# Splitting the first projection by columns and reordering the start of an attention-plus-gMLP kernel

## The chip, the cores and the metric

The kernel runs on one core of a Trainium2 chip. The metric is the device time of one execution in microseconds (us). A core has five engines that run their own instruction streams: TensorE (PE; its weight loads are shown apart as PEld), VectorE (DVE), ScalarE (ACT), GpSimd (POOL) and SyncE (SP). Here SP and POOL mostly issue transfers; ACT issues a few as well.

## The reference

The input `x` has 2048 rows of 1024 bf16 numbers. Two blocks follow each other: sliding attention, and a gated MLP that also mixes over the rows.

```python
h  = x + A(layernorm(x), wqkv, wo)
h2 = h + B(layernorm(h), w_in, w_sp, b_sp, w_out)

def A(x, wqkv, wo):                       # 32 heads of 32
    q, k, v = split(x @ wqkv)
    idx  = pos[:, None] - 2 * arange(8)   # 8 keys per row, two rows apart, looking back
    logits = einsum('bhsd,bhswd->bhsw', q, k[idx]) * 32 ** -0.5   # idx < 0 masked
    o = einsum('bhsw,bhswd->bhsd', softmax(logits), v[idx])
    return o @ wo

def B(x, w_in, w_sp, b_sp, w_out):
    z1, z2 = halves(gelu(x @ w_in))       # 1792 columns each
    z2 = layernorm(z2)
    g  = w_sp @ z2 + b_sp[:, None]        # 2048 x 2048, mixes rows
    return (z1 * g) @ w_out
```

## The kernel before

**Tiling.** The rows are worked in four chunks of 512 (`CH`), each of four tiles of 128 rows (`TPC`). A matmul contracts over 128 partitions, so 1024 columns are eight slices (`KT`), and a 128x512 matmul fills half of a PSUM accumulator `acc` (three of them; one more PSUM region, `L`, belongs to attention). Q, k and v are computed transposed (columns of wqkv on the partitions, rows of x along the free axis): a chunk of q is 64 matmuls in four accumulators of 16. Column `m*8+dl` of q goes to partition `m`, slice `dl`, so the weights of a matmul are read with a stride of eight columns.

**Stages.** In the first (up to about 438 us) the chunks pass through LN1, q/k/v, attention, the wo projection with the residual and LN2 (`head`), and the two halves of the gelu projection (`b_z2`, `b_z1`), interleaved. In the second, z2 of all 16 tiles sits in SBUF, and per chunk there are the spatial product with w_sp (L810) and the projection by w_out (L825).

**What sets the order.** From `qkv(0)` on, nearly every piece of work of the first stage is handed to `Order` (L63, used as `o_` from L282) as an operation with an engine, an estimated duration, its dependencies and a priority; `take` and `free` name buffers. `Order.run` simulates the engines with these estimates and then emits the operations in the order of their simulated starts, so it fixes each engine's instruction order. A "DMA" operation is either a transfer to be issued (by SP, `dma`, or by POOL, `dma_w`) or a mere delay. What comes ahead of that (the start, L206 to L271) is placed by the framework's own scheduler. Each engine, and each queue of transfers, then works its stream in order and waits for semaphores.

**The start.** PE runs 14 warm-up matmuls on a zeroed tile (L207, L210). Tiles 0 and 3 of x are loaded by SP and ACT (L214: SP loads 0 and 3, ACT 1 and 2), then wq in eight slices (L217), wk (L218), x of chunk 1 by tiles (L220), wv (L221) and x of chunks 2 and 3 (L223), all on SP. DVE takes mean and variance of tiles 0, 1, 2 (`stats`, L227 to L229), ACT those of tile 3 by two sums over the tile (`stats_act`, L234/L235, finished on DVE, L236 to L238); ACT takes the root (L242), DVE the reciprocal (L243) and the normed tile (`norm`, L247). PE turns a tile by eight 128x128 transposes into PSUM (L255), and one copy of 128x1024 brings it to `xnT[0]` (L256; ACT, but DVE for tile 2). Then q of chunk 0: the first 32 matmuls go over the slices `kt` on the outside and four column groups on the inside, in two accumulators (L346), the other 32 are normal groups (L355); ACT brings accumulators out (L362).

**LN1 of chunks 1 to 3** (`ln1`, L294): statistics on DVE, `rstd` by a power on POOL (L303), four norms on DVE, each stored to a buffer `xn_d` in DRAM by POOL's queue (L309); then one DMA transpose on SP from `xn_d` to `xnT[c]` (L315). Matmuls of q, k, v follow (L355); ACT copies each accumulator to a staging tile (L367), and SP stores it to `qkv_d` in DRAM.

**Attention** (`attention`, L378). POOL's queue loads `qT`, `kT` and `vT` of the chunk from `qkv_d` (L387; chunk 0 has them in SBUF), kT and vT with 16 rows of the chunk before. The load of qT waits for `qfree` of the chunk before, that of kT for `qkdone`, that of vT for `avdone`. For each of eight windows DVE multiplies qT with the shifted kT (L414, into one of two buffers `prod`) and adds slices up (L418, L421, L424) into `part`. After four windows PE sums over each head's partitions with four matmuls into `L` (L442, at most one half of `L` a visit), so there are two visits a chunk. Softmax is on DVE and ACT (L451 to L485), PE spreads the weights over the partitions again (`pb`, L497), copies bring them to `AB` (L502). DVE multiplies v with AB for each window (L517) and adds (L525); two of the sums are done by accumulating transfers on POOL's queue (`gather`, L531), `av_y<-av_z` and `av_oT<-av_zz`. The product `z` is kept in the buffer of qT (`homes`, L508), so `qfree` is the end of the first of these transfers (L536).

**Head and gMLP.** `head`: wo projection (L587), residual with x loaded once more (`xr`, L591; L596), squares (L601), LN2 (L629), and a DMA transpose of the normed tiles `hb` on SP into `hnT` (L634; for the last chunk by tiles, L619). `b_z2` (L660) and `b_z1` (L710) are matmuls that depend only on `hnT` and on weights; where no attention work is ready for PE, `Order` puts them there.

Of the kernel before, what the change touches and what calls it, by code (L numbers as in the profile page):

```python
# [20 lines left out]
P = 128  # L21
NT = S // P
# [10 lines left out]
NWARM = 14  # L33
# [4 lines left out]
ACCUM_US = 12.0  # L38
PIECES = ((0, 0), (0, 4), (1, 0), (1, 4))
LNPRIO = (0, 2.0, 2.5, 4.0)  # L40
# [86 lines left out]
def kernel(  # L127
# [18 lines left out]

    consts_d = nc.inline_tensor(_consts(), name="qt_consts")
# [6 lines left out]
    xn_d = {c: dpool.tile([CH, D], BF16, name=f"xn_d{c}") for c in (1, 2, 3)}  # L154
# [9 lines left out]
    V.memset(eps_t[:], EPS)  # L164
    texp = cpool.tile([P, 1], FP32, name="texp")
    nhalf = cpool.tile([P, TPC], FP32, name="nhalf")
    V.memset(nhalf[:], -0.5)
# [34 lines left out]
    def load_x(i):  # L202
        x_slot(i)
        dma(xts[i], x2d[i * P:(i + 1) * P, :])
# [4 lines left out]
    for _ in range(NWARM):  # L209
        T.matmul(wps[:], warm[:, 0:P], warm[:], start=True, stop=True)  # L210

    for i in (0, 3, 1, 2):
        x_slot(i)
# [17 lines left out]
    def stats_act(i):  # L231
        sm = l1.tile([P, 4], FP32, name="sm", tag="sm")
        jk = l1.tile([P, D], BF16, name="jk", tag="xn", bufs=4)
        A.activation(jk[:], xts[i], ACTF.Identity, accum_out=sm[:, 0:1])  # L234
        A.activation(jk[:], xts[i], ACTF.Square, accum_out=sm[:, 1:2])  # L235
# [4 lines left out]
    def rstd_of(lo, hi):  # L240
# [4 lines left out]
    def norm(i):  # L245
        xn = l1.tile([P, D], BF16, name="xn", tag="xn", bufs=4)
        V.tensor_scalar(xn[:], xts[i], mv1[:, i, 0:1], rstd1[:, i:i + 1], op0=ALU.subtract, op1=ALU.mult)  # L247
        return xn

    xnT[0] = xtp.tile([P, KT, CH], BF16, name="xnT", tag="xnT")  # L250

    def xpose(i, xn):
        tp = ps_acc.tile([P, KT, P], BF16, name="tpa", tag="acc")
        for a in range(KT):
            T.transpose(tp[:, a, :], xn[:, a * P:(a + 1) * P], ident)  # L255
        (V.tensor_copy if i == 2 else A.copy)(xnT[0][:, :, i * P:(i + 1) * P], tp[:])  # L256
# [3 lines left out]
    stats_act(3)  # L260
    stats(V, 0)
    rstd_of(0, 1)
    stats(V, 1)
    xpose(0, norm(0))
    rstd_of(1, 2)
    rstd_of(3, 4)
    xpose(1, norm(1))
    xpose(3, norm(3))
    stats(V, 2)
    rstd_of(2, 3)  # L270
    xpose(2, norm(2))  # L271
# [10 lines left out]
    o_ = Order({"PE": 12.9, "ACT": 12.0, "DVE": 12.6, "POOL": 12.0}, {"acc": 3, "L": 1, "prod": 2, "part": 2, "xn": 4})  # L282
# [8 lines left out]
    X_AT = {1: 18.5, 2: 27.5, 3: 30.5}  # L291
    xn_ready = {}

    def ln1(c):  # L294
        sts = []
        for i in range(c * TPC, (c + 1) * TPC):
            arrive = add("DMA", X_AT[c] + 0.8 * (i % TPC), lambda: None)
            sts.append(add("DVE", 1.32, lambda i=i: stats(V, i), [arrive], prio=LNPRIO[c]))
# [572 lines left out]
```

## Time and profile before

| what | value |
|---|---|
| median of 3 runs | 732.07 us (731.43 to 734.21) |
| the profiled execution | 734.07 us, of which the span from first to last instruction 732.2 |
| granted TensorE clock, mean | 0.995 |
| DVE, ACT, POOL busy | 419.3 (57%), 220.8 (30%), 59.0 (8%) us |
| from 0 to 28.64 us (to the end of chunk 0's q) | PE busy 24.57, at a mean granted clock of 0.88; DMA share 0.96, 350 GB/s |
| from 28.64 to 438.70 (rest of the first stage) | PE busy 408.33 of 410.06; DVE 329.31; DMA share 0.69 |
| from 438.70 to the end | PE busy 290.30 of 293.50; DVE 73.49; ACT 1.02; DMA share 0.27 |
| HBM read, written | 55.09 MB, 33.88 MB |

The profiled execution is 2.0 us above the median of the runs; all positions in the trace belong to it. The stages differ: in the last one almost only PE works, and what a change does there is a shift of the whole; up to 28.64 us PE has unoccupied time and a lowered clock; in between, PE and DVE both have long streams that meet at a few places in each chunk.

### The profile page before, as it was taken

What the parts mean: (1) busy time and instruction counts of PE and PEld (TensorE: products, weight loads), DVE (VectorE), ACT (ScalarE), POOL (GpSimd) and SP (SyncE); (2) the same over time, 40 slices, a digit from 0 to 9 for tenths busy, and PEclk for the clock granted to TensorE, in tenths of its full rate; (3) what the DMA queues carried; (4) which work ended last, traced back from release to release, by engine and by line L of the source; (5) the groups of instructions that cost most, each with busy time, mean ns of one, the idle gap of its engine ahead of it and who ended that gap; (6) DMA issues with size and microseconds to landing.
All of it is one profiled execution on the core that took longest, in us unless ns stands there. A gap on an engine that the chain in (4) does not pass through costs nothing.

```text
span 732.2 us, 8410 instructions
## 1 busy us (share of the span) xinstructions
PE 723.2 (99%) x3452; PEld 367.1 (50%) x3452; DVE 419.3 (57%) x464; ACT 220.8 (30%) x269; POOL 59.0 (8%) x74
## 2 busy tenths in 40 slices
PE   7999999999999999999999999999999999999998
PEld 3666665566645344444444444444444444444444
DVE  4889999999899899989940101322232223222322
ACT  4322522544238874678654620000000000000000
POOL 0310110001201110201203000000000000000000
PEclk8999999999999999999999999999999999999999
DMA  9874398476993485383569898344105311020002
GB/s 338 311 263 112 124 235 253 145 187 204 317 372 66 150 214 166 101 233 64 123 195 295 191 283 259 111 114 131 58 30 127 117 57 42 22 90 21 1 16 71
DMA packets 115398, 113.64 MB, mean 155 GB/s; under 512 B 67904, under 2 KB 91872, under 8 KB 115232
## 3 DMA queue, kind: packets, MB, share of 16 engines
q1 hardware_dynamic: 105472, 72.63, 33.9%
q0 software_dynamic: 9456, 39.89, 18.7%
q8 instruction: 27, 0.44, 0.2%
q10 hardware_dynamic: 432, 0.59, 0.2%
q14 instruction: 11, 0.09, 0.0%
HBM read 55.09 MB, written 33.88 MB: 122 GB/s over the span
## 4 chain that ended last, share of the span: by engine, by line
PE 89%; DMA 5%; DVE 4%; issue 1%; ACT 0%; DVEq 0%
PE acc L810 26%; PE acc L355 18%; PE acc L825 13%; PE acc L710 13%; PE acc L660 10%; PE acc L587 6%; DMA qT<-qkv_d 2%; DVE prod L414 2%; DMA qkv_d<-stg 2%; PE acc L346 1%; DMA xr<-in_A_x_dram 1%; DVE prod L418 1%; DVE prod L421 0%; DMA xp<-in_A_x_dram 0%; PE tpa L255 0%
## 5 line engine op out<-in xcount | busy, mean ns | idle before, releaser
L810 PE MATMUL acc<-wspT,z2sb 128*128 128x512 bf16 x896 | 194.0, 379 | 0.0
L810 PEld LDWEIGHTS <-z2sb 128*128 128x128 bf16 x896 | 87.7, 98 | 105.7
L813 DVE TENSOR_TENSOR g<-acc,bB 128x1024 bf16<-128x1024 f32 x28 | 34.3, 1224 | 160.2 <-PE acc L810 127.6
L660 PE MATMUL acc<-win,hnT 128*128 128x512 bf16 (+1 forms) x512 | 98.5, 352 | 0.0
L710 PE MATMUL acc<-hnT,win 128*128 128x512 bf16 x448 | 98.4, 379 | 0.0
L414 DVE TENSOR_TENSOR prod<-qT,kT 128x4096 bf16<-128x4096 bf16 x32 | 72.5, 2283 | 5.2 <-ACT kT L362 2.9
L660 PEld LDWEIGHTS <-hnT 128*128 128x128 bf16 x512 | 49.8, 98 | 47.3 <-issue 0.7
L825 PEld LDWEIGHTS <-zg 128*128 128x128 bf16 x462 | 45.2, 98 | 51.8
L710 PEld LDWEIGHTS <-win 128*128 128x128 bf16 x448 | 43.4, 98 | 52.4 <-issue 1.1
L367 ACT CAST stg<-acc 128x1024 bf16<-128x1024 f32 x36 | 36.4, 1011 | 72.7 <-PE acc L355 59.2
L825 PE MATMUL acc<-wout_a,zg 128*128 128x512 bf16 (+1 forms) x264 | 58.2, 373 | 0.0
L832 DVE TENSOR_TENSOR ot<-acc,hr 128x1024 bf16<-128x1024 f32 x15 | 18.4, 1225 | 69.4 <-PE acc L825 69.4
L355 PE MATMUL acc<-xnT,wv 128*128 128x512 bf16 x256 | 56.6, 380 | 0.0
L355 PE MATMUL acc<-xnT,wk 128*128 128x512 bf16 x256 | 56.3, 379 | 0.0
L587 PE MATMUL acc<-wo_sb,av_oT 128*128 128x512 bf16 x256 | 55.9, 379 | 0.0
L355 PE MATMUL acc<-xnT,wq 128*128 128x512 bf16 x224 | 49.7, 380 | 0.0
L355 PEld LDWEIGHTS <-wk 128*128 128x128 bf16 x256 | 36.5, 144 | 18.8 <-issue 0.5
L355 PEld LDWEIGHTS <-wv 128*128 128x128 bf16 x256 | 36.5, 144 | 18.8 <-issue 0.7
L825 PE MATMUL acc<-wout_b,zg 128*128 128x512 bf16 (+1 forms) x198 | 44.4, 373 | 0.0
L587 PEld LDWEIGHTS <-av_oT 128*128 128x128 bf16 x256 | 25.1, 98 | 30.1
L355 PEld LDWEIGHTS <-wq 128*128 128x128 bf16 x224 | 31.9, 144 | 16.4 <-issue 0.7
L418 DVE TENSOR_TENSOR prod<-prod 128x2048 bf16<-128x2048 bf16 x32 | 38.3, 1216 | 0.0
(135 smaller groups left out, 565.0 us busy)
## 6 DMA issues: line engine op xcount, KB each, us to landing
qkv_d<-stg SPq DMA_DIRECT2D x36, 256.0 KB, 3.2
z_d<-z1s SPq DMA_DIRECT2D x28, 256.0 KB, 3.5
z1c<-z_d SPq DMA_DIRECT2D x28, 256.0 KB, 2.6
z_d<-u SPq DMA_DIRECT2D x12, 448.0 KB, 4.2
z2sb<-z_d POOLq DMA_DIRECT2D x12, 448.0 KB, 15.6
xr<-in_A_x_dram SPq DMA_DIRECT2D x16, 256.0 KB, 2.8
av_y<-av_z POOLq DMA_DIRECT2D x4, 1024.0 KB, 10.0
av_oT<-av_zz POOLq DMA_DIRECT2D x4, 1024.0 KB, 13.4
```

What stands on the lines that cost most here:

```text
L346: T.matmul(accs[dl // 2][:, dl % 2, :], wv[:, kt, dl, :], xnT[0][:, kt, :], start=(kt == 0), stop=(kt == KT - 1))
L355: T.matmul(G[key][:, j, :], wv[:, kt, dl, :], xnT[c][:, kt, :], start=(kt == 0), stop=(kt == KT - 1))
L367: A.copy(stg[:], G[key][:])
L414: V.tensor_tensor(st["prod"][:], qT[:], kT[:, :, o:o + CH], op=ALU.mult)
L418: V.tensor_tensor(dst, p_[:, 0:4, :], p_[:, 4:8, :], op=ALU.add)
L587: T.matmul(st["acc", il][:, nh, :], oTs[c][:, dl, il * P:(il + 1) * P], wo_sb[:, dl, nh * CH:(nh + 1) * CH], start=(dl == 0), stop=(dl == ...
L660: T.matmul(accf[:, n0:n1], hnTs[c][:, il, kt, :], wins[hf][:, kt, n0:n1], start=(kt == 0), stop=(kt == KT - 1))
L710: T.matmul(G["accy", c, fp][:, j, :].rearrange("p (a b) -> p a b", a=TPC), wt[:, kt, f0 * P:(f0 + 1) * P], hnTs[c][:, :, kt, :], start=(kt ...
L810: T.matmul(acc[:, j, :], z2sb[a][:, f * P:(f + 1) * P], wspT[:, a, :], start=(a == 0), stop=(a == NT - 1))
L813: V.tensor_tensor(g1[:], acc[:], bB[:, c * CH:(c + 1) * CH].unsqueeze(1).to_broadcast([P, 2, CH]), op=ALU.add)
L825: T.matmul(outs, zg[:, f, il * P:(il + 1) * P], wt[:, f0, lo:hi], start=(f == 0), stop=(f == NF - 1))
L832: V.tensor_tensor(ot[:], acc[:].rearrange("p a b -> p (a b)"), hr[:], op=ALU.add)
```

## The change

The start is written out by hand for all engines, and some of the later work is placed differently.

- **Start.** 20 warm-up matmuls in place of 14. Tiles 0 and 1 of x are loaded in column halves, one by SP and one by ACT; tile 2 by SP, tile 3 by ACT. Each tile's transposes go to a PSUM region of its own, and its copy out is two 128x512 copies by one engine: even tiles ACT, odd tiles DVE. For the first 32 matmuls of q, the left half of the rows (tiles 0 and 1) is done by 128x256 matmuls before tiles 2 and 3 are turned, the right half after that; the other 32 are full ones. `xnT` is laid out by tiles.
- **Loads of x.** Chunks 1 and 2 come in pairs of tiles, two pairs ahead of wk and two behind it; chunk 3 comes in one load (`xl`) ahead of wv, into a buffer of the products (`prod`), so `Order` starts with one `prod` buffer and gets the other when chunk 3's norms are done.
- **LN1 of chunks 1 to 3.** The normed tiles go to a buffer `xns` in SBUF, and the DMA transpose reads that; `xn_d` and its stores are gone. The buffers `hn0` and `hn1` are shared by `xns`, `hnT` and the product `z`; `xns` of chunk 3 takes the one of chunk 1 and waits for its transpose. ACT sums tiles 7 and 11, finished on DVE.
- **Head sums.** `part` holds all eight windows; eight matmuls in one visit of PE per chunk.
- **Product z.** Chunks 0 and 1 keep it in `hn1`, so the next chunk's qT is loaded once the products with qT are done (`qkdone`).
- **The planner's numbers.** Starts of the engines, arrival times of x, due times of the accumulating transfers (11 and 15 in place of 12), some durations and priorities.

```diff
-NWARM = 14
+NWARM = 20
...
-ACCUM_US = 12.0
 PIECES = ((0, 0), (0, 4), (1, 0), (1, 4))
-LNPRIO = (0, 2.0, 2.5, 4.0)
+LNPRIO = (0, 2.0, 2.5, 2.8)
...
+    by_hand = tc.manual_schedule(engines={mybir.EngineType.PE, mybir.EngineType.Activation, mybir.EngineType.DVE, mybir.EngineType.Pool})
+    by_hand.__enter__()
...
-    xn_d = {c: dpool.tile([CH, D], BF16, name=f"xn_d{c}") for c in (1, 2, 3)}
...
+    def load_pair(k):
+        x_slot(2 * k)
+        x_slot(2 * k + 1)
+        dma(pairs[k][:], x2d[2 * k * P:(2 * k + 2) * P, :].rearrange("(t p) d -> p t d", p=P))
...
-    for i in (0, 3, 1, 2):
-        x_slot(i)
-        (dma if i < 2 else A.dma_start)(xts[i], x2d[i * P:(i + 1) * P, :])
...
-    for kt in range(KT):
-        dma(wsb[0][:, kt, :], wq_view[:, kt, 0:D])
-    dma(wsb[1][:], wq_view[:, :, D:2 * D])
-    for i in range(TPC, 2 * TPC):
-        load_x(i)
-    dma(wsb[2][:], wq_view[:, :, 2 * D:3 * D])
-    for i in range(2 * TPC, NT):
-        load_x(i)
+    with tc.manual_schedule(engines={mybir.EngineType.SP}):
+        for i in range(TPC):
+            x_slot(i)
+        for i in range(2):
+            for q_, lo in ((nc.sync, 0), (nc.scalar, CH)):
+                q_.dma_start(xts[i][:, lo:lo + CH], x2d[i * P:(i + 1) * P, lo:lo + CH])
+        dma(xts[2], x2d[2 * P:3 * P, :])
+        A.dma_start(xts[3], x2d[3 * P:4 * P, :])
+        for kt in range(KT):
+            dma(wsb[0][:, kt, :], wq_view[:, kt, 0:D])
+        load_pair(2)
+        load_pair(3)
+        dma(wsb[1][:], wq_view[:, :, D:2 * D])
+        load_pair(4)
+        load_pair(5)
+        xl = att.tile([P, TPC, D], BF16, name="xl", tag="prod", bufs=2)
+        dma(xl[:], x2d[3 * CH:4 * CH, :].rearrange("(t p) d -> p t d", p=P))
+        for i in range(TPC):
+            xts[3 * TPC + i] = xl[:, i, :]
+        dma(wsb[2][:], wq_view[:, :, 2 * D:3 * D])
...
+    def stats_half(i, hf, st=None):
+        if hf == 0:
+            st = l1.tile([P, 2, 6], FP32, name="bnst", tag="bnst")
+        V.bn_stats(st[:, hf, :], xts[i][:, hf * CH:(hf + 1) * CH])
+        if hf:
+            V.bn_aggr(mv1[:, i, :], st[:])
+        return st
+
+    def sums_act(i, k, junk, sm=None):
+        if k == 0:
+            sm = l1.tile([P, 4], FP32, name="sm", tag="sm")
+        A.activation(junk, xts[i], (ACTF.Identity, ACTF.Square)[k], accum_out=sm[:, k:k + 1])
+        return sm
+
...
+    def root(lo, hi):
         sd = l1.tile([P, TPC], FP32, name="sd1", tag="sd1")
         A.activation(sd[:, 0:hi - lo], mv1[:, lo:hi, 1], ACTF.Sqrt, bias=eps_t[:])
-        V.reciprocal(rstd1[:, lo:hi], sd[:, 0:hi - lo])
...
+        return sd
...
+    def norm(i, out=None):
...
+    xnT[0] = xtp.tile([P, TPC, KT, P], BF16, name="xnT", tag="xnT")
...
+    xns = {c: bp.tile([P, TPC, D], BF16, name=f"xns{c}", tag=f"hn{c - 1}", bufs=1) for c in (1, 2)}
...
     def xpose(i, xn):
-        tp = ps_acc.tile([P, KT, P], BF16, name="tpa", tag="acc")
+        tps[i] = ps_acc.tile([P, 2, 2 * CH], BF16, name="tpb", tag="acc") if i % 2 else ps_att.tile([P, 2, 2 * CH], BF16, name="tpa", tag="L")
         for a in range(KT):
-            T.transpose(tp[:, a, :], xn[:, a * P:(a + 1) * P], ident)
-        (V.tensor_copy if i == 2 else A.copy)(xnT[0][:, :, i * P:(i + 1) * P], tp[:])
+            T.transpose(tps[i][:, a // 4, (a % 4) * P:(a % 4 + 1) * P], xn[:, a * P:(a + 1) * P], ident)
+
+    def xput(i):
+        for hf in range(2):
+            (V.tensor_copy if i % 2 else A.copy)(xnT[0][:, i, 4 * hf:4 * hf + 4, :], tps[i][:, hf, 0:CH].rearrange("p (a s) -> p a s", a=4))
+
+    def q_mm(dl, kt, lo, hi):
+        T.matmul(qacc[dl // 2][:, dl % 2, lo * P:hi * P].rearrange("p (a b) -> p a b", b=P), wqs[:, kt, dl, :], xnT[0][:, lo:hi, kt, :],
+                 start=(kt == 0), stop=(kt == KT - 1))
+
+    def q_left(lo, hi):
+        for kt in range(lo, hi):
+            for dl in range(4):
+                q_mm(dl, kt, 0, 2)
+
+    def q_out(dp):
+        A.copy(att_in[0][0][:, 2 * dp:2 * dp + 2, :], qacc[dp][:])
...
-    stats_act(3)
     stats(V, 0)
-    rstd_of(0, 1)
+    sd0 = root(0, 1)
     stats(V, 1)
-    xpose(0, norm(0))
...
-    xpose(2, norm(2))
+    sd1 = root(1, 2)
+    sm = sums_act(3, 0, junk())
+    V.reciprocal(rstd1[:, 0:1], sd0[:, 0:1])
+    xn = {0: norm(0)}
+    V.reciprocal(rstd1[:, 1:2], sd1[:, 0:1])
+    xn[1] = norm(1)
+    xpose(0, xn[0])
+    xput(0)
+    st2 = stats_half(2, 0)
+    xpose(1, xn[1])
+    xput(1)
+    stats_half(2, 1, st2)
+    sums_act(3, 1, junk(), sm)
+    sd2 = root(2, 3)
+    var_act(3, sm)
+    sd3 = root(3, 4)
+    V.reciprocal(rstd1[:, 2:3], sd2[:, 0:1])
+    xn[2] = norm(2)
+    V.reciprocal(rstd1[:, 3:4], sd3[:, 0:1])
+    xn[3] = norm(3)
+    qacc[0], qacc[1] = new_acc(), new_acc()
+    q_left(0, 6)
+    xpose(2, xn[2])
+    xput(2)
+    xpose(3, xn[3])
+    xput(3)
+    q_left(6, KT)
+    sm7 = sums_act(7, 0, junk())
+    sums_act(7, 1, junk(), sm7)
+    for dp in range(2):
+        for dl in (2 * dp, 2 * dp + 1):
+            for kt in range(KT):
+                q_mm(dl, kt, 2, TPC)
+        q_out(dp)
+    for dp in (2, 3):
+        qacc[dp] = new_acc()
+        for dl in (2 * dp, 2 * dp + 1):
+            for kt in range(KT):
+                q_mm(dl, kt, 0, TPC)
+        q_out(dp)
...
-    o_ = Order({"PE": 12.9, "ACT": 12.0, "DVE": 12.6, "POOL": 12.0}, {"acc": 3, "L": 1, "prod": 2, "part": 2, "xn": 4})
+    o_ = Order({"PE": 24.9, "ACT": 26.0, "DVE": 14.4, "POOL": 12.0}, {"acc": 3, "L": 1, "prod": 1, "part": 2, "xn": 4})
...
+        for il in range(TPC):
+            i = c * TPC + il
+            arrive = add("DMA", X_AT[c] + 0.8 * il, lambda: None)
+            if il < TPC - 1 or c == 3:
+                sts.append(add("DVE", 1.4, lambda i=i: stats(V, i), [arrive], prio=LNPRIO[c]))
+                continue
+            if c == 1:
+                G["sm", c] = sm7
+                sa = add("DMA", 17.5, lambda: None)
+            else:
...
+                    G["sm", c] = sums_act(i, 0, junk())
+                    sums_act(i, 1, junk(), G["sm", c])
+                sa = add("ACT", 2.4, sums, [arrive], prio=4.0, lat=0.2)
+            sts.append(add("DVE", 0.45, lambda i=i: var_act(i, G["sm", c]), [sa], prio=LNPRIO[c]))
...
-        ns = []
-        for il in range(TPC):
-            def nrm(i=c * TPC + il, il=il):
-                xn = norm(i)
-                dma_w(xn_d[c][il * P:(il + 1) * P, :], xn[:])
-            n_ = add("DVE", 0.48, nrm, [r1], prio=LNPRIO[c] - 0.5, take="xn")
-            ns.append(dma_op(4.0, lambda: None, [n_], free="xn"))
-            G["xns"] = G.get("xns", []) + [n_]
+        def nrm(il):
+            if c == 3 and il == 0:
+                xns[c] = bp.tile([P, TPC, D], BF16, name="xns3", tag="hn0", bufs=1)
+            norm(c * TPC + il, xns[c][:, il, :])
+        ns = [add("DVE", 0.48, lambda il=il: nrm(il), [r1] + ([G["xnT", 1]] if c == 3 else []), prio=LNPRIO[c] - 0.5,
+                  free="prod" if c == 3 and il == TPC - 1 else None) for il in range(TPC)]
+        G["normed", c] = ns[-1]
         def tr():
-            xnT[c] = xtp.tile([P, KT, CH], BF16, name="xnT", tag="xnT")
-            i_ = nc.sync.dma_start_transpose(xnT[c][:], xn_d[c].rearrange("s (a p) -> s a p", p=P))
+            xnT[c] = xtp.tile([P, TPC, KT, P], BF16, name="xnT", tag="xnT")
+            i_ = nc.sync.dma_start_transpose(xnT[c][:].rearrange("p il a s -> p (il a) s"), xns[c][:].rearrange("s il (a p) -> s (il a) p", p=P))
             if c == 3:
                 tc.add_manual_dep(i_.ins, G["vload", 1].ins.name, wait_for, reason="keep the xbar transpose out of the sums and loads")
-        G["xnT", c] = dma_op(8.0, tr, ns + ([G["qkvlast", c - 2]] if c >= 2 else []))
...
+        G["xnT", c] = dma_op(9.0, tr, ns + ([G["qkvlast", c - 2]] if c >= 2 else []))
...
-        for xi in range(3):
+        for xi in range(0 if c else 1, 3):
...
+                    def mm(j=j, k0=k0, dl=2 * dp + j, wv=wv, key=key):
...
+                            T.matmul(G[key][:, j, :].rearrange("p (a b) -> p a b", a=TPC), wv[:, kt, dl, :], xnT[c][:, :, kt, :],
+                                     start=(kt == 0), stop=(kt == KT - 1))
...
-            d_q = dma_op(7.0, ld(0), ev[0:4] + [G["qfree", c - 1]] + (G["xns"] if c == 1 else []))
+            d_q = dma_op(7.0, ld(0), ev[0:4] + [G["qfree", c - 1]] )
...
-        nw = 8 // max(mode, 2)
+        nw = 8 // mode
...
+                n = min(nw, 4)
                 for z in range(mode):
-                    for sq in range(4):
-                        T.matmul(L[32 * sq:32 * sq + 32, nw * g:nw * g + nw, :], E32,
-                                 parts[g][:, :, z, sq * P:(sq + 1) * P],
-                                 start=(z == 0), stop=(z == mode - 1), tile_position=(0, 32 * sq))
-            lms.append(add("PE", {1: 0.38, 2: 0.65, 4: 0.65}[mode], lm, [slack], prio=1.0, take="L" if g == 0 else None, free="part", lat=0.2))
+                    for w0 in range(0, nw, n):
+                        for sq in range(4):
+                            T.matmul(L[32 * sq:32 * sq + 32, nw * g + w0:nw * g + w0 + n, :], E32,
+                                     parts[g][:, w0:w0 + n, z, sq * P:(sq + 1) * P],
+                                     start=(z == 0), stop=(z == mode - 1), tile_position=(0, 32 * sq))
+            lms.append(add("PE", 0.92 if mode == 1 else 0.75, lm, [slack], prio=1.0, take="L" if g == 0 else None, free="part", lat=0.2))
...
-        homes = {"y": (att, "part", 2), "z": (att, "qT", 1), "zz": (bp, "hb", 1), "b": (att, "prod", 2), "p": (att, "prod", 2), "oT": (att, "oT", 1)}
+        homes = {"y": (att, "part", 2), "z": (bp, "hn1", 1) if c < 2 else (att, "qT", 1), "zz": (bp, "hb", 1), "b": (att, "prod", 2), "p": (att, "prod", 2), "oT": (att, "oT", 1)}
...
-        def gather(to, key, deps):
+        def gather(to, key, deps, us):
...
-        g1 = G["qfree", c] = gather("y", "z", [z])
+        g1 = gather("y", "z", [z], 11.0)
+        G["qfree", c] = g1 if c == 2 else G["qkdone", c]
...
-        g2 = gather("oT", "zz", [z])
+        g2 = gather("oT", "zz", [z], 15.0)
...
-            hnTs[c] = bp.tile([P, TPC, KT, P], BF16, name="hnT", tag="hnT")
+            hnTs[c] = bp.tile([P, TPC, KT, P], BF16, name="hnT", tag="hn%d" % (c % 2), bufs=1)
```

More of the change, by code (lines that the diff above doesn't have):

```diff
@@ new lines, in qkv @@
+                for j, k0 in PIECES:
+                    def mm(j=j, k0=k0, dl=2 * dp + j, wv=wv, key=key):
+                        if j == 0 and k0 == 0:
+                            G[key] = new_acc()
+                        for kt in range(k0, k0 + 4):
+                            T.matmul(G[key][:, j, :].rearrange("p (a b) -> p a b", a=TPC), wv[:, kt, dl, :], xnT[c][:, :, kt, :],
+                                     start=(kt == 0), stop=(kt == KT - 1))
+                    last = add("PE", 0.863, mm, deps, prio=order(), take="acc" if j == 0 and k0 == 0 else None)
+                    deps = [(last, 0.0)]
@@ L786 @@
     dma_op(0.0, wsp0, [G["z1ev", NCH - 2], G["close"], zl_])
-    with tc.manual_schedule(engines={mybir.EngineType.PE, mybir.EngineType.Activation, mybir.EngineType.DVE, mybir.EngineType.Pool}):
-        o_.run()
-        wout_a = wtile([P, 8, D], "wout_a", "wA")
-        wout_b = wtile([P, NF - 8, D], "wout_b", "wA")
-        wout_view = B_w_out.rearrange("(f p) n -> p f n", p=P)
-        for i_ in (dma_w(wout_a[:], wout_view[:, 0:8, :]), dma_w(wout_b[:], wout_view[:, 8:NF, :])):
-            tc.add_manual_dep(i_.ins, wsp_ins[0].ins.name, wait_for, reason="keep the load out of the xbar transpose")
+    o_.run()
+    wout_a = wtile([P, 8, D], "wout_a", "wA")
+    wout_b = wtile([P, NF - 8, D], "wout_b", "wA")
+    wout_view = B_w_out.rearrange("(f p) n -> p f n", p=P)
+    for i_ in (dma_w(wout_a[:], wout_view[:, 0:8, :]), dma_w(wout_b[:], wout_view[:, 8:NF, :])):
+        tc.add_manual_dep(i_.ins, wsp_ins[0].ins.name, wait_for, reason="keep the load out of the xbar transpose")
+    by_hand.__exit__(None, None, None)
     t2.close()
```

85 lines of the change are left out of this document (25 added, 60 removed).

## The prediction

> **What bounds the kernel now.** I read the page first: the busy line and the clock row.
>
> ```profile
> PE 723.2 (99%) x3452; PEld 367.1 (50%) x3452; DVE 419.3 (57%) x464; ACT 220.8 (30%) x269; POOL 59.0 (8%) x74
> ...
> PEclk8999999999999999999999999999999999999999
> ```
>
> TensorE (PE) is busy for all but 9.0 us of the 732.2. Nothing can be won by making another engine faster unless PE waits for it, so the next view is what PE waits for.
>
> ```profile
> PE tpa L255 <- DVE xn L247: 1.9, 1, 1.9
> PE L L442 <- DVE part L424: 1.7, 2, 1.5
> PE wps L210 <- DVE warm L207: 1.3, 1, 1.3
> PE acc L346 <- DVE xnT L256: 0.9, 1, 0.9
> ```
>
> Three of the four are in the start, the fourth (1.7) is at the head sums of L442. But "busy" hides time: the timeline of PE in the first 30 us has warm-up, transposes and a slow first group.
>
> ```profile
> 1.25 5.79 PE L210 MATMUL wps<-warm 128*128 128x512 bf16 x14 [1.25 <-DVE warm L207]
> 8.95 3.11 PE L255 MATMUL tpa<-csb,xn 128*128 128x128 bf16 x32 [1.91 <-DVE xn L247]
> 12.93 8.97 PE L346 MATMUL acc<-xnT,wq 128*128 128x512 bf16 x32 [0.88 <-DVE xnT L256]
> 21.73 7.07 PE L355 MATMUL acc<-xnT,wq 128*128 128x512 bf16 x32
> ```
>
> The second 32 query matmuls start at 21.73 and the next group at 28.64: 6.91, or 0.216 each. The first 32 take 8.8. The windows view says why (after the engines' busy times come granted clock, DMA share and GB/s).
>
> ```profile
> 6.50:9.90 3.40, 1.46 (x17) 0.76 (x16) 3.40 (x13) 1.61 (x7) 0.00 (x0) 1.00 1.05 387
> 9.90:13.30 3.40, 2.52 (x23) 2.10 (x21) 1.41 (x4) 2.54 (x3) 0.00 (x0) 0.51 1.04 386
> 13.30:16.70 3.40, 3.40 (x9) 1.31 (x8) 0.00 (x0) 0.00 (x0) 0.00 (x0) 0.50 1.04 387
> ```
>
> From 9.9 to 16.7 the clock is at half, and nine matmuls take 0.427 each: 1.9 us lost. So the q stage ends at 28.64 of which 13.8 is work at full rate. From there to the last matmul PE runs in one piece, save L442. The chain of waits shows where the longer of its two waits (1.54 at 242.15) comes from.
>
> ```profile
> 175.37 11.61 DMA qkv_d<-stg
> 187.15 13.68 DMA qT<-qkv_d
> 200.88 2.17 issue
> 203.06 2.29 DVE prod L414
> ...
> 241.67 0.43 DVE part L424
> 242.15 0.40 PE L L442 x4
> ```
>
> Chunk 2's q is loaded late, VectorE (DVE) waits 2.29 for it (198.55 to 200.84), works 41 us with one pause of 1.43, and PE waits at the end of that.
>
> **The q stage of chunk 0, from 28.64 to 25.1.** Each step as the instructions of the changed kernel stand on their engines:
> - x tile 0 comes in halves over two queues, ahead of tile 3; it lands at 4.32 now. Bounds 4.0 and 4.35; I take 4.2.
> - Statistics of tiles 0 and 1 on DVE: 1.44 a tile (17.59 to 19.03), so 7.1; reciprocal 0.15 and norm 0.55 give tile 0 at 7.8, tile 1 at 8.4.
> - Warm-up is 20 matmuls from about 1.1: 0.427 each until 6.5, then 0.216, so to 8.1. The transposes follow it with no gap: 16 in two eights of 0.62, of which the last 0.17 overlaps, to 9.2.
> - Copies out: ScalarE (ACT) two halves. No row has 128x512 from bf16; 128x1024 takes 1.02 (bounds 0.5 and 0.81, the 768-column row of L667); at 0.55 each, 8.7 to 9.8. DVE two halves at 0.35 (half of L256's 0.69; at most 0.69), after one statistics call, 9.3 to 10.0. The left half of q starts at 10.1, in place of 12.93.
> - Half matmuls: 128x256 with strided weights is in no row. With plain weights such matmuls follow each other every 0.109 (L825's eight from 725.78 to 726.65). Strided weights take 144 ns to load, plain ones 98, so 0.144 is the upper bound. I take 0.109: eight transposes, each with a 98 ns load, took 0.62 in all, so loads overlap each other. 24 halves to 12.7; tiles 2 and 3 are normed at about 12.4 and 13.1 (ACT's two sums of tile 3, 1.06 + 0.19 each, come between), transposed by 13.6; 8 halves to 14.5; DVE's copy to 14.4; 32 halves of the right side, 3.5, to 18.1; 32 full ones, 6.9, to 25.0, and 0.1 for two hand-overs.
> Gain 3.5; with 0.144 a half it is 1.3, with x at 4.0 and no hand-overs 4.0.
>
> **The loads behind it** cost nothing while two covers hold. At the 387 GB/s of the windows from about 2.9, wk ends at 19.3 and is wanted at 25.1; wv ends at 30 and is wanted at 38.9. Without cover each us late is a us. Chunk 1's x lands at 13.9 instead of 17.6.
>
> **Head sums once per chunk** (8 matmuls in one visit, at L442's place): a visit costs 0.33, and 0.15 of way in and out (32 matmuls before one end 0.09 ahead of it, and 36 from 70.57 take 7.86 to the next). Eight become four. Where the second four stream behind the first for 0.22, a chunk saves 0.26, where they take 0.33 it saves 0.15: I put 0.8 on the four; bounds 0 (each four costs a visit) and 1.0.
>
> **LN1 on chip, one-engine copies, x of chunk 3 in a product buffer.** Twelve 256 KB stores leave POOL's queue (0.575 each), and the transposes read SBUF: hnT<-hb already does so, 6.7 to 8.4 to landing, against 5.7 to 9.0 for xnT<-xn_d. PE wants chunk 1's at 52.7; normed at about 23, it has 30 us. So zero. Chunk 3's four norms leave the softmax of chunk 0, where they cost DVE 0.93, and stand before its first products. There they wait for chunk 1's transpose, whose source they overwrite; all of DVE is queued behind. ACT takes the sums of tiles 7 and 11 (2.5 each) next to q's copies: the first ends at 16.9, and q's first copy, ready at 16.4, then holds a PSUM buffer until 17.9; PE wants it at 18.1.
>
> **q loads earlier.** The z product of chunks 0 and 1 moves out of q's buffer, so the next q is loaded once the products are done. On POOL's queue qT now stands ahead of kT, which stands ahead of the sums av_y: qT can go at 74, kT at 86 (its k is stored then), av_y at 90, so nobody is held. DVE's 2.29 at 200.84 goes, and with it PE's two waits at L442: 1.7, and 0.1 for the second's hand-over, so 1.8; bounds 0, if DVE is as late for another reason, and 1.9.
>
> **New waits.** One sum at the very end of each chunk's products means PE meets DVE there. DVE's products start 1.2 after k's last matmul (40.1); last part 34.2 later (43.70 to 77.92), 74.3; PE arrives after 232 matmuls of 0.216, at 75.2. Counting on with the durations of before (41.0, 41.2 and 41.8 for the later chunks' products, 29.6 for the weighted sums) PE comes 1.1, 1.8 and 0.8 after DVE, and 0.9 to 1.5 after it at the four wo stages. All small, none negative; I put 0.3 on it. If DVE lost x us, PE would lose x minus about 0.9, once.
>
> **Sum.** -3.5 - 0.8 - 1.8 + 0.3 = -5.8. The profiled execution took 734.07 (span 732.2 and 1.9 around it), so 728.3 for one like it; the median of the runs, 732.07, is 2.0 below the profiled one, and I carry that distance over: **726.3**.
>
> **Rivals.**
> 1. The clock falls to half within q. After 6.5 to 9.9, with 0.5 of warm-up and about 1 us of transposes, it was halved; 2.1 of transposes and 0.4 of matmuls in the next stretch did not bring it back; it was back at 16.8, 3.9 after steady matmuls began. In the new order 8.1 to 10.1 holds transposes alone. Against it: those 2 us are less than one such stretch. If it falls, 24 halves cost 0.213 instead of 0.109: 2.5, so 728.8. The Trainium skill (TensorE: Matmul & The Clock Gate, Part 1) has the clock halve only after an idle window of about 3.4 us, in windows that run freely, and Part 4 adds that transposes do not count as busy; the trace agrees on transposes, while its drop followed a window with 0.5 us of matmuls in it. By that rule the clock stays up here and the time stays 726.3.
> 2. The gain is given back to DVE: the four meetings cost 0.8 each, because stores, loads or sums of a chunk take longer than their rows. For it: slacks of 0.8 to 1.8 are thin. Against: the one long wait for a load is removed. 726.3 + 3.2 = 729.5.
> 3. The halves do not do what they should: 0.144 each, 728.5.
> 4. Slower: chunk 1's transpose is late, and chunk 3's norms hold DVE. It is issued at about 23 on the queue that still carries wv until 30. It decides from a landing at 38.2 on (four norms, 1.9, then the products at 40.1); from 45 all is given back. If it only starts behind wv, needs its 4.9 of issue (L634) and then 13.7 as the q load of 187.15 did: 48.6, so 10.4 late, minus 0.9, plus the sum: 732.07 - 5.8 + 9.5 = 735.8. Against it: every transpose here landed in 9.0 or less, so 39. The Trainium skill (DMA: Bandwidth & Descriptors, Two DMAs through the same engine are not ordered) says that descriptors of one queue start in order, which puts it behind wv; no row of before has the two together.
>
> **Chances.** Forecast 0.58, own range 724.8 to 728.2; rival 1 0.13, rival 2 0.14, rival 3 0.07, rival 4 0.08. Half a percent, about what a measurement of this kernel can tell, is 3.7 us: 728.4. All of the forecast, and what of 1 and 3 falls below that line, are faster: 0.68. Same 0.22, slower 0.10 (rival 4 and accidents). Range 724.6 to 731.0: below, 4.0 for q, 1.0 for the sums and 1.9 for the waits with none new, and 0.6 of scatter as between the runs of before; above, rivals 1 to 3, with rival 4 left out.
>
> **What would show it.** Right: first 128x256 matmul near 10.1, every 0.109, last q matmul near 25; clock 1.00 from 6.5; L's waits under 0.5 in all; prod not waiting for qT; the third stage (the spatial product) starting near 433 instead of 438.7. Wrong: halves every 0.144, clock 0.5 within 10 to 17, xns norms of chunk 3 waiting for DMA past 38, or PE waits at the sums of more than 1 us each.

## The result, and the profile after

| | median, us | runs | profiled execution |
|---|---|---|---|
| before | 732.18 (731.43 to 734.21) | 6 | 734.07, span 732.2, clock 0.995 |
| changed | 727.24 (726.95 to 727.64) | 6 | 727.23, span 725.4, clock 1.0 |

The ratio is 0.9928, 95% interval [0.9916, 0.9939]: 4.9 us faster, where 726.3 (5.8 faster) was forecast. The page of the changed kernel, busy line and clock row:

```profile
PE 718.2 (99%) x3445; PEld 369.1 (51%) x3490; DVE 420.1 (58%) x467; ACT 224.7 (31%) x278; POOL 54.0 (7%) x62
...
PEclk9999999999999999999999999999999999999999
```

PE is still the bound, with 7.2 us of the span not busy in place of 9.0. The first slice of the clock row is now a 9. What PE waits for (engine, line, releaser: us in total, times, longest):

```profile
PE wps L209 <- DVE eps_t L210: 1.2, 1, 1.2
PE acc L284 <- DVE xnT L281: 0.6, 1, 0.6
```

The first is at the very start, the second ahead of the first half matmul. The wait at the head sums (1.7) is gone, and so is the one of 1.9 ahead of the first transposes: the longer warm-up now fills that time. The timeline of PE (start, us, line, operation, count):

```profile
8.49 0.61 PE L277 MATMUL tpa<-csb,xn 128*128 128x128 bf16 x8
8.93 0.61 PE L277 MATMUL tpb<-csb,xn 128*128 128x128 bf16 x8
10.15 2.81 PE L284 MATMUL acc<-xnT,wq 128*128 128x256 bf16 x24 [0.61 <-DVE xnT L281]
...
13.69 11.44 PE L284 MATMUL acc<-xnT,wq 128*128 128x256 bf16 x72
24.97 5.34 PE L433 MATMUL acc<-xnT,wk 128*128 128x512 bf16 x24
```

The first half matmul starts at 10.15 (10.1 forecast), 24 of them take until 12.80, which is 0.110 each, and k begins at 24.97 (25.1 forecast). The chain of waits (start, us, what) is nearly all PE now (99% of it, 89% before), without the transfers and DVE work of before; three of its pieces:

```profile
13.85 11.28 PE acc L284 x72
25.14 50.07 PE acc L433 x232
75.75 7.93 PE acc L433 x36
```

From one profile to the other the q stage ends 3.7 sooner (28.64 to 24.97), the rest of the first stage is 2.9 shorter (the third stage starts at 432.12 instead of 438.70; about 433 was forecast), and the last stage is the same within 0.2. That makes 6.8, not 4.9: the profiled execution of before lay 1.9 above its median, the profiled one of the changed kernel on it. The experiments begin there.

### The profile page after: what moved, and what is told of

It reads as the page before. It is cut to its first block, busy times and chain, and to the rows that moved or that the text cites. A ratio compares the mean times of both kernels' runs of the same rounds, so it can differ in the third digit from the quotient of the medians.

```text
span 725.4 us, 8425 instructions
## 1 busy us (share of the span) xinstructions
PE 718.2 (99%) x3445; PEld 369.1 (51%) x3490; DVE 420.1 (58%) x467; ACT 224.7 (31%) x278; POOL 54.0 (7%) x62
## 4 chain that ended last, share of the span: by engine, by line
PE 99%; issue 0%; DVE 0%
PE acc L886 27%; PE acc L433 21%; PE acc L790 13%; PE acc L740 13%; PE acc L901 13%; PE acc L667 8%; PE acc L284 2%; PE wps L209 1%; PE pb L576 0%; PE L L521 0%; PE tpa L277 0%; PE tpb L277 0%; DVE xnT L281 0%; DVE ot L915 0%; DVE warm L206 0%
## 5 line engine op out<-in xcount | busy, mean ns | idle before, releaser
L740 PE MATMUL acc<-win,hnT 128*128 128x512 bf16 (+1 forms) x500 | 97.7, 352 | 0.6
L740 PEld LDWEIGHTS <-hnT 128*128 128x128 bf16 x512 | 49.8, 98 | 47.6 <-issue 0.9
L433 PE MATMUL acc<-xnT,wq 128*128 128x512 bf16 x192 | 42.4, 380 | 0.0
L747 ACT ACTIVATE u<-acc 128x1024 bf16<-128x1024 f32 (+1 forms) x32 | 29.3, 916 | 29.0 <-PE acc L740 28.7
```

The lines of the kernel that those rows point to most:

```text
L433: T.matmul(G[key][:, j, :].rearrange("p (a b) -> p a b", a=TPC), wv[:, kt, dl, :], xnT[c][:, :, kt, :], start=(kt == 0), stop=(kt == KT - 1))
L740: T.matmul(accf[:, n0:n1], hnTs[c][:, il, kt, :], wins[hf][:, kt, n0:n1], start=(kt == 0), stop=(kt == KT - 1))
L747: A.activation(st["u", il][:, hf * 1024:hf * 1024 + wd], G["accz", c, il, hf][:].rearrange("p a b -> p (a b)")[:, 0:wd], ACTF.Gelu_apprx_t ...
```

## The experiments

All medians are in us. The median is that of all executions of a kernel; the other columns belong to its one profiled execution, which can lie off the median (731.18 for "q not split", 728.83 for "two visits"). "Rest" is the span less the end of chunk 0's q, so it leaves the start out.

| kernel | median | q ends | rest | PE waits at the sums | DVE waits for qT |
|---|---|---|---|---|---|
| before, first profile | 732.18 | 28.64 | 703.6 | 1.7 | 2.3 |
| before, again | 732.66 | 26.43 | 703.9 | 2.0 | 2.2 |
| before, 20 warm-ups | 731.77 | 26.36 | 703.2 | 1.5 | 2.3 |
| before, z apart | 730.58 | 26.93 | 701.6 | 0 | 0 |
| before, one visit | 729.94 | 26.14 | 701.8 | 0.9 | 2.6 |
| changed | 727.24 | 24.97 | 700.4 | 0 | 0 |
| changed, again | 726.70 | 24.16 | 700.3 | 0 | 0 |
| changed, two visits | 728.11 | 25.23 | 701.5 | 0 | 0 |
| changed, z in qT | 726.59 | 25.06 | 700.3 | 0 | 0.8 |
| changed, both of these | 729.33 | 24.74 | 702.5 | 1.1 | 2.4 |
| changed, q not split | 732.39 | 28.95 | 700.4 | 0 | 0 |
| changed, 14 warm-ups | 726.18 | 23.89 | 700.4 | 0 | 0 |
| changed, 10 warm-ups | 728.82 | 23.87 | 703.0 | 0 | 0 |
| changed, x of chunk 1 late | 732.60 | 30.59 | 700.4 | 0 | 0 |

### Why the profiled execution of before was slow

The kernel before once more, without an edit.

> The kernel before, unchanged, for a second profiled execution. The first one took 734.07, 1.9 above the median of its runs (732.18), the changed kernel's profiled one lies on its median (727.23 against 727.24). Theory: the 1.9 is something that the change removes and that differs from run to run, PE's wait at the head sums of L442 behind the late load of qT (1.86 in the first profile). Then an execution near 732 has less than 0.5 of it, its q stage ends at 28.6 all the same, and the clock is at half from about 10 to 17. Rival: the stretch at half clock differs: the waits at L442 are again 1.9 in all, and the q stage ends up to 1.9 earlier. Second rival: neither, both are as in the first profile and the scatter lies in the last stage. Time: 732.0 to 732.4 median in all cases.

Its profiled execution took 732.15. PE's timeline, and then what PE waits for:

```profile
12.62 7.07 PE L346 MATMUL acc<-xnT,wq 128*128 128x512 bf16 x32 [1.17 <-ACT xnT L256]
19.52 7.07 PE L355 MATMUL acc<-xnT,wq 128*128 128x512 bf16 x32
26.43 5.77 PE L355 MATMUL acc<-xnT,wk 128*128 128x512 bf16 x26
```

```profile
PE L L442 <- DVE part L424: 2.0, 2, 1.5
```

The rival holds. The wait is there again, and the first 32 q matmuls take 6.9 in place of 8.8: the clock, once up, did not fall. Over 76 executions of this kernel the time goes with the mean granted clock: 1.0 in 28 of them (median 731.8), 0.997 or 0.998 in 33 (732.5 and 732.7), 0.995 in 12 (734.1), 0.993 in 3 (735.4). So q of the kernel before ends at 26.4 or later, and its first profile was one of the slower kind (15 of the 76 had a clock of 0.995 or less).

### The warm-up, and what lets the clock fall

The kernel before, with one constant changed:

```diff
-NWARM = 14
+NWARM = 20
```

> The kernel before with 20 warm-up matmuls in place of 14 and nothing else, so the warm-up ends at 8.3 instead of 7.0, ahead of the first transposes at 8.95. Theory of the prediction's rival 1: the clock fell at 9.95 because the stretch before it held only 0.5 us of matmuls; with 1.8 in it, the clock stays at 1.0 and the first 32 q matmuls take 0.216 each in place of 0.27 on average: 1.9 less, 730.3. Rival: it falls anyway, at the transposes, since 9.9 to 12.9 has no matmul in either kernel: 732.2, no change.

Measured 731.77, ratio to before 0.9989 [0.9980, 0.9997]; all 11 executions at a clock of 0.999 or 1.0. The longer warm-up does keep the clock up, but the median execution of before (732.36 beside it) loses only about 0.6 by it, not the 1.9 of its first profile; at a clock of 1.0 the two kernels are equal (731.80 and 731.79).

In these traces the granted clock changes only at steps of 3.41 us or multiples of it (from 9.95 to 16.77 are two), whose position differs from execution to execution (in before's first profile 6.53, 9.95, 16.77; in others 4.52 or 7.03). Three views of such steps (window: us, PE busy, PEld, DVE, ACT, POOL busy, granted clock, DMA share, GB/s): before's first profile, then the two kernels "z apart" and "one visit" of below, which have the same start.

```profile
6.53:9.95 3.42, 1.48 (x18) 0.81 (x16) 3.42 (x14) 1.63 (x7) 0.00 (x0) 1.00 1.05 388
9.95:13.36 3.41, 2.54 (x23) 2.06 (x21) 1.35 (x4) 2.50 (x3) 0.00 (x0) 0.50 1.05 387
13.36:16.77 3.41, 3.41 (x10) 1.30 (x9) 0.00 (x0) 0.00 (x0) 0.00 (x0) 0.50 1.04 387
```

```profile
6.11:9.53 3.42, 1.39 (x13) 0.60 (x11) 3.42 (x16) 1.67 (x7) 0.00 (x0) 1.00 1.05 387
9.53:12.94 3.41, 2.68 (x24) 2.41 (x24) 1.66 (x4) 2.89 (x3) 0.00 (x0) 0.50 1.05 387
12.94:16.35 3.41, 3.27 (x15) 2.22 (x16) 0.00 (x0) 0.00 (x0) 0.00 (x0) 1.00 1.05 387
```

```profile
7.52:10.93 3.41, 2.08 (x31) 1.74 (x32) 2.93 (x12) 2.27 (x5) 0.00 (x0) 1.00 1.06 390
10.93:14.34 3.41, 2.25 (x15) 1.57 (x13) 0.69 (x1) 1.34 (x2) 0.00 (x0) 1.00 1.04 386
```

Read each line's PE busy time against the clock of the line below it. After 1.48 and 1.39 the clock was at half, after 2.08 it stayed up; at half, 2.54 did not bring it back and 2.68 did. The 2.08 and the 2.68 are transposes alone, so transposes without a matmul can hold the clock and raise it. Three further traces fit. A step with 0.74 us of work ("q not split", 9.30 to 12.72) and one with none ("x of chunk 1 late", 21.96 to 25.37) were followed by half clock, and in the second profile of the kernel before a step with 1.52 was not:

```profile
4.52:7.93 3.41, 1.52 (x7) 0.49 (x5) 3.41 (x12) 2.48 (x5) 0.00 (x0) 1.00 1.05 395
7.93:11.34 3.41, 2.21 (x32) 1.80 (x32) 2.81 (x10) 2.39 (x5) 0.00 (x0) 1.00 1.05 386
```

So the clock fell after steps of up to 1.48 and not after steps of 1.52 and more, and rose from half after 2.68 but not after 2.54. That PE's busy time alone decides is a reading of these steps; no run varied it by itself, and 1.48 and 1.52 are close for a busy time whose ends are modelled.

The changed kernel, 14 warm-ups:

```diff
-NWARM = 20
+NWARM = 14
```

> The changed kernel with 14 warm-up matmuls in place of 20: the warm-up ends at 7.0, and until the first half matmul near 10.0 there are only transposes. If a gap like that of the kernel before is enough to lower the clock, it falls at about 10, comes back about 17, and matmuls of 3.4 us at full rate take twice that: 730.6. If 3 us without matmuls are not enough, the clock stays at 1.00 and the time at 727.2, or up to 0.6 less, since the first transposes no longer stand behind the warm-up (8.49, with tile 0 normed at 7.17).

Measured 726.18 (four executions, 726.13 to 726.34, all at a clock of 1.0), ratio to before 0.9915 [0.9902, 0.9928]. Its executions lie below every one of the changed kernel (726.38 is the lowest of those), but the two were not measured beside each other, and the intervals of their ratios overlap (0.9928 [0.9916, 0.9939] for the changed kernel), so a gain over it is likely but not shown. Its PE timeline:

```profile
7.17 0.62 PE L277 MATMUL tpa<-csb,xn 128*128 128x128 bf16 x8 [1.21 <-DVE xn L267]
7.83 0.62 PE L277 MATMUL tpb<-csb,xn 128*128 128x128 bf16 x8
9.06 2.81 PE L284 MATMUL acc<-xnT,wq 128*128 128x256 bf16 x24 [0.61 <-DVE xnT L281]
```

The transposes start with the normed tile (7.17), not behind the warm-up (8.49), and all of q is 1.1 earlier. With 20, how long the warm-up lasts hangs on when the clock rises: in the changed kernel's first profile it rose at 6.78 and the transposes started at 8.49, in its second (below) at 4.00 and 7.16. Four executions do not show that the clock holds at every position of its steps.

The changed kernel unchanged, measured beside the other experiments on it:

> The changed kernel, unchanged, as the measure for the others of this call. No theory differs on it: 727.2, and the clock at 1.00 in all executions if the matmuls of the new order are dense enough at any position of the clock's 3.41 us windows; an execution with 0.998 would show that they are not.

726.70 (726.38 to 727.26, five executions, clock 1.0 in all), 5.6 below the kernel before beside it (732.29). And 10 warm-ups (`NWARM = 10`):

> The changed kernel with 10 warm-up matmuls, to find where a shorter warm-up begins to cost. With 14 PE met tile 0's first transpose without a wait behind the warm-up (7.17) and the time was 726.2. Theory: 10 at half clock end at 5.5 at the latest; the clock rises only after a 3.41 us window that is busy for more than 2.5, and falls after one with less than 1.5 to 2.1, so at some positions of the window it does not rise before q, or falls during the transposes: some executions at 726.2 with a granted clock of 1.00, others 1.7 to 3.4 longer with 0.995 to 0.998; median about 727.5. Rival: the transposes keep it up, and all executions lie at 726.2.

728.82 (726.14 to 733.09), granted clocks of 0.995, 0.997, 0.998 and 1.0 in 3, 1, 3 and 2 of nine executions. So 10 are too few. The two slowest lie 6.0 and 6.9 above the fastest, more than the 3.4 that was expected of the clock; why is open. The profiled one, at a clock of 1.0, has a wait that no other run shows: PE at L740 for the last tile's transpose `hnT<-hb`, 2.5, which took 20.9 to land. That alone is nothing unusual: it took 16.3 in the changed kernel and 21.8 in the kernel before, where PE did not wait for it. Whether the earlier start brings the wait on or chance is open.

### The split of q

The changed kernel with q of chunk 0 in full matmuls, behind all four tiles:

```diff
-    q_left(0, 6)
     xpose(2, xn[2])
...
-    q_left(6, KT)
+    for kt in range(KT):
+        for dl in range(4):
+            q_mm(dl, kt, 0, TPC)
...
```

> The changed kernel with q of chunk 0 not split by columns: 32 full matmuls of 128x512 wait for all four tiles (copied out at 14.65 in the changed kernel), then the other 32. Theory: the split is most of the 3.7 won in the start. From 14.7 on 64 matmuls of 0.216 are 13.8, so the q stage ends at 28.5 in place of 24.97: 730.8 with the clock at 1.00. If the clock also falls over the stretch 8.3 to 14.7, in which there are only transposes, up to 1.9 more: 732.7. Rival: the loads and copies moved ahead are most of it, and the time stays below 728.5.

Measured 732.39; the clock fell in all 12 executions (0.995 in nine). The q stage of the profiled one, the fastest of the 12, ends at 28.95, with the clock at half from 12.72 to 16.13. The theory holds: with the loads and copies moved but no split, the start is no better than before. The split does two things at once: it uses the time in which tiles 2 and 3 are still being normed, and it fills the steps of the clock. This run takes both away together. An estimate parts them: the 64 q matmuls take 14.8 in place of 13.8 and the last eight transposes 0.96 in place of 0.61, so the clock costs about 1.3 of the 4.0 by which q ends later.

### Head sums and the load of q

The changed kernel with two visits a chunk (and the planner's old estimate of 0.38 a visit), then with z back in the buffer of qT:

```diff
-        nw = 8 // mode
+        nw = 8 // max(mode, 2)
```

> The changed kernel with the head sums in two visits a chunk of four matmuls each, as before. Theory: each extra visit costs only its way in and out, 0.095 and 0.106 us in the traces, so four cost 0.8: 728.0. Rival: a visit also costs a stream of 0.22 (eight matmuls of two visits in place of two groups in one), so 4 x 0.42 = 1.7: 728.9. Second rival: PE has slack against DVE at the visits and they cost nothing that shows: 727.2.

```diff
-        homes = {"y": (att, "part", 2), "z": (bp, "hn1", 1) if c < 2 else (att, "qT", 1), "zz": (bp, "hb", 1), "b": (att, "prod", 2), "p": (att, "prod", 2), "oT": (att, "oT", 1)}
+        homes = {"y": (att, "part", 2), "z": (att, "qT", 1), "zz": (bp, "hb", 1), "b": (att, "prod", 2), "p": (att, "prod", 2), "oT": (att, "oT", 1)}
...
-        G["qfree", c] = g1 if c == 2 else G["qkdone", c]
+        G["qfree", c] = g1
```

> The changed kernel with the product z of all chunks back in the buffer of qT, so that the next chunk's qT is loaded only when the first accumulating transfer is done. Theory: this is what made DVE wait 2.3 for chunk 2's qT and PE 1.9 to 2.0 at the head sums in both profiles of the kernel before; with one visit a chunk PE meets DVE at the last part, so it waits 1.0 to 2.0 in all: 728.2 to 729.2, and the wait shows as PE L behind DVE part. Rival: the late load came from the stores of the normed tiles and the two visits, which stay away here: DVE does not wait, 727.2.

Two visits: 728.11, 1.4 more than the changed kernel beside it; by the rest of its profile, which leaves out the scatter of the start, 1.1 more. PE has no wait at the sums. That is nearer the theory (0.8) than the rival (1.7). About 0.2 of the other 0.3 shows in the starts of its matmuls: the first full matmul behind a visit takes 0.27 in place of 0.22 in chunks 0 and 1, and at chunk 2's second visit PE starts 0.1 later than elsewhere, since DVE's last part is done only then (236.93, the visit starts at 236.97). z in qT: 726.59, no difference. DVE does wait for qT, by one line of what it waits for:

```profile
DVE prod L491 <- DMA qT<-qkv_d: 0.8, 1, 0.8
```

but PE comes 0.7 after DVE's last part at chunk 2's sums, as in the changed kernel. Alone, then, the earlier load of q is worth nothing there. Whether it is what ended the wait, three more kernels tell. First both parts taken back together:

> The changed kernel with both parts taken back: two visits a chunk and z in the buffer of qT. Theory: each of the two covers the other, and each alone left no PE wait; with both gone DVE's 0.8 to 1.0 at the load of chunk 2's qT comes out at PE's second visit, where the two-visit kernel had PE arrive just as DVE was done: 728.1 + 0.9 = 729.0, with a PE wait of about 0.9 at the head sums. Rival: there is no wait, 728.1, and the kernel before lost its 2 us by something else that the change moved.

729.33, and the waits are back, PE's and DVE's:

```profile
PE L L521 <- DVE part L501: 1.1, 1, 1.1
```

```profile
DVE prod L491 <- DMA qT<-qkv_d: 2.4, 1, 2.4
```

Then each part alone in the kernel before. For z apart, `homes` is as in the change, and hnT gets the two buffers hn0 and hn1.

```diff
-        g1 = G["qfree", c] = gather("y", "z", [z])
+        g1 = gather("y", "z", [z])
+        G["qfree", c] = g1 if c == 2 else G["qkdone", c]
...
-            hnTs[c] = bp.tile([P, TPC, KT, P], BF16, name="hnT", tag="hnT")
+            hnTs[c] = bp.tile([P, TPC, KT, P], BF16, name="hnT", tag="hn%d" % (c % 2), bufs=1)
```

> The kernel before with one part of the change: the product z of chunks 0 and 1 in a buffer of its own (hn1, shared with hnT), so qT of the next chunk is loaded as soon as its products are done. The planner's order of the instructions is the same as before. Theory (the prediction's step on the q loads): DVE no longer waits 2.2 for chunk 2's qT, and PE's 1.9 to 2.0 at the head sums goes: 730.3, no PE wait at L442 over 0.3, the same times at every clock. Rival: something else on DVE is as late (its products of chunk 2 take 41.8 in place of the planned 39.7), and PE still waits 1.0 or more: 731.3 to 732.3.

730.58, ratio 0.9974 [0.9961, 0.9986]: 2.1 less, no wait of DVE for qT and no PE wait at the sums. The load of q was the cause of DVE's wait, and that of PE's. For one visit, the matmuls of L442 run in two groups of four windows as in the change, at a planned 0.92 a visit.

```diff
-        nw = 8 // max(mode, 2)
+        nw = 8 // mode
```

> The kernel before with one part of the change: all eight windows in one part tile and the head sums in one visit a chunk. The q load stays behind the accumulating transfer. Theory: the sums save 0.85 by themselves, and since the planner, which plans with its own longer estimates, then sets PE's only visit of chunk 2 some 3 us later (240.99 in place of 237.68 by its estimates), PE meets DVE after the 2.2 that DVE loses at the load, so the wait goes as well: 732.3 - 0.85 - 1.9 = 729.5, although DVE still waits for qT. Rival: the visit stands where DVE's last part ends and the 2.2 come out there: PE waits 2.0 once more, 731.4.

729.94, ratio 0.9959 [0.9944, 0.9974]: 2.7 less. DVE still waits 2.6 for qT, but PE, whose only visit the planner puts later against DVE, waits 0.9 in place of 2.0. So the one removes PE's wait by its cause, the other about half of it by moving the meeting, and their gains, 2.1 and 2.7, do not add up: from 703.9 the rest goes to 701.6 with one, to 701.8 with the other, to 700.4 with both and all else.

### The cover of the loads

The changed kernel with x of chunk 1 behind wk:

```diff
-        load_pair(2)
-        load_pair(3)
         dma(wsb[1][:], wq_view[:, :, D:2 * D])
+        load_pair(2)
+        load_pair(3)
```

> The changed kernel with x of chunk 1 loaded behind wk in place of ahead of it: it lands about 5.4 later (2 MB at 387 GB/s), so chunk 1's normed tiles stand at about 26.5 and its transpose is issued then, in place of 22.9. Theory (rival 4 of the prediction): chunk 3's norms wait for that transpose; if it takes 14.1 to land as in the changed kernel, they start at 40.6 in place of 37.65, DVE's first product at 42.7 in place of 40.0, and PE, 0.8 behind DVE at chunk 0's head sums, loses 1.9 there, once: 729.1. Rival: the transpose lands sooner when it starts later, since less of wv is left in front of it; then it lands at about 37 all the same, and the time stays at 727.2.

732.60, worse than either theory. The transpose did what the rival said: issued at 29.18, it landed within 7.6, at 36.8. But PE lost time much earlier, by its waits and by the timeline of ACT:

```profile
PE acc L284 <- ACT qT L293: 4.0, 1, 4.0
```

```profile
22.43 1.06 ACT L252 ACTIVATE jk<-xp 128x1024 bf16<-128x1024 bf16 x1 [8.03 <-DMA xp<-in_A_x_dram]
...
24.52 2.81 ACT L293 CAST qT<-acc 128x1024 bf16<-128x1024 f32 x3
```

ACT's sums over tile 7 stand ahead of q's first copy in ACT's stream. While they wait for x, PE has no accumulator to go on with; the granted clock was below 1.0 in 11 of 12 executions. In the profiled one the clock was at half from 25.37 to 28.79, after the step without work. All of the loss is in the q stage (30.59 against 24.97; the rest is 700.4). In the changed kernel the same copy could start at 16.4, runs at 18.17 to 19.2, and PE goes on into the fourth accumulator at 21.5, so that the cover is 2.3.

## Why the prediction was right, and where it was off

- **q stage, -3.5:** -3.67 between the two profiles, and the steps stood near their places (10.15, 0.110 a half, 24.97). The size is right only against that execution of before: against one at full clock (26.43) it is 1.5 to 2.3 (24.97, 24.16). What stands ahead of the prediction has the first loads of the kernel before wrong: by L214 SP loads tiles 0 and 1, ACT tiles 3 and 2, so tile 0 already led its queue, and the halves only share it between two.
- **Sums once per chunk, -0.8:** the starts of the matmuls give 0.8 (0.094 into and 0.106 out of each of four visits), the run with two visits 1.1 by its rest.
- **q loads earlier, -1.8:** right in cause for the kernel before (z apart: -2.1, no wait left). It was costed as if it alone removed the wait; the single visit removes half of it as well, and in the changed kernel all of it.
- **New waits, +0.3:** 0. PE comes 0.8, 1.0, 0.7 and 1.1 after DVE at the four sums, where 0.9, 1.1, 1.8 and 0.8 were counted: the third is 1.1 too high, but none is negative, and PE waits for none.
- **Loads, 0; LN1 on chip, 0:** the traces show no wait for them, but a cover was named in the wrong place: late x of chunk 1 costs through ACT's queue and q's copies before it costs through the transpose. Both of ACT's sums stand ahead of q's first copy (18.17, not 16.9), and PE came for the freed buffer at 21.5, not 18.1. LN1 through DRAM was not tried apart.
- **The step that failed** is the last: "the median of the runs, 732.07, is 2.0 below the profiled one, and I carry that distance over". That distance was not common to both kernels. It was the clock at half from 9.95 to 16.77 (2.2 by the ends of q, 28.64 and 26.43), which is what the change takes away, and it had been booked in the q term already. The sum itself came out at 728.3 and the profiled execution at 727.23, 1.1 less: 0.3 for new waits that are not there, 0.2 in q, 0.1 in sums and waits, and some 0.4 in the rest and at the end that no step named. The two errors are of opposite sign and leave 0.9, and that is luck. So is the size of the sum: between the two second profiles, both at full clock (span 730.3 and 724.5), the gain is 5.8 as well, but of 2.3 in the q stage and 3.5 in the rest, where 3.5 and 2.3 were forecast.
- **Rivals.** 1 (clock falls): it did not, in any of 11 executions (0.999 or 1.0). The page of the Trainium skill (TensorE: Matmul & The Clock Gate, Part 1) was right on windows that run freely, but no window had to be idle: 0.74, 1.39 and 1.48 us of work let the clock fall too. Its Part 4, that a transpose does not count as busy in the same way, and the prediction's "the trace agrees on transposes" differ from the 2.08 and 2.68 above. 2 and 3 are excluded by the waits and by the 0.110. 4: the transpose of chunk 1 took 14.1 to land, more than the 9.0 argued, and was down at about 37.0, only 1.2 ahead of the point from which it decides; started later it was faster. The argument that every transpose of the kernel before landed in 9.0 or less was a misreading: it left out those of the last chunk's tiles, one of which took 21.8 in the same profile.

## What to carry to other kernels

Before a gain is read against a median, ask why the profiled execution differs from it: an excess that the change removes must not be carried over to the other side. A warm-up that lasts longer than the first real work takes to get ready delays that work (8.49 against 7.17 here), one that is too short lets the clock fall in some executions; in these traces transposes held the clock as matmuls did. Where two edits remove the same wait, undoing one shows nothing; undo both, or make each alone in the old kernel.

## What was not expected of the hardware

- PE transposes kept the clock up by themselves (2.08 us of them in a step of 3.41) and raised it from half (2.68); 1.48 of work let it fall, 1.52 did not, and 2.54 did not raise it.
- The DMA transpose of the same tiles took 14.1 to land when issued at 22.88 and 7.6 when issued at 29.18. Both were issued before wv, which stands ahead of them on the queue, was down (33.5 and 33.3), and both landed 3.5 after it.
- The transpose of the last chunk's last tile took 13.9 to 21.8 to land in all 14 profiles, those of the other three tiles 5.2 at most.
- Each visit of PE to the narrow head sums costs about 0.2 on top of its matmuls (0.094 before the first, 0.106 after the last).
